# Two attention and state-space layer pairs on one core: one region of fixed order over the whole program, new order strings, six normalisations and some evictions on other engines

## The chip, the cores and the metric

The kernel runs on one core of a Trainium2 chip. The metric is device time in microseconds: 395.22 is the median of three runs of the kernel before (394.33 to 395.49). The core's engines are named as in the profile: PE (TensorE, matmuls; PEld are its weight loads), DVE (VectorE), ACT (ScalarE), POOL (GpSimd) and SP (SyncE, which here issues nearly all DMAs). Each engine works through a queue of its own, in order, and waits on semaphores for the others.

## What is computed

The input `x` is 1 x 2048 x 512. Four residual layers follow each other, attention A and convolution B by turns:

```python
x = x + A(layernorm(x))      # then  x + B(layernorm(x)), and both once more
# A: 32 heads of 16, every position attends to 8 positions, 2 apart, behind it
qkv = x @ wqkv
logits = einsum("bhsd,bhswd->bhsw", q, kg) * scale     # masked, softmax over w
o = einsum("bhsw,bhswd->bhsd", attn, vg) @ wo
# B: a state-space layer as a long convolution
P = exp(dt * A * l);  K = einsum("dn,dnl,dn->dl", C, P, dt * B).real
y = irfft(rfft(u, 2L) * rfft(K, 2L))[:L] + u * Dskip
```

Both A layers share their weights, and both B layers their kernel `K` and so its spectrum.

## The kernel before

The program has these stages, one after the other; the times in brackets are where DVE works on them in the profiled execution.

- **Generator**, `k_gen` (0.9 to 101.3 us). It builds the tables from which `K` comes: a complex number per state is squared again and again (`square` on ACT, L1087; `double` and `differ` on DVE, L1091 and L1094; tile `sq_z`), the powers are copied out in bf16 (L1105, L1107, L1111), products of tables are made on DVE (L1119) and summed on PE (L1277). Between these stand table steps on ACT (L661, L684), the first layernorm of layer 0 (row statistics L145 and L1163, application `ln_apply` L195 on ACT or L197 on DVE and POOL), transposes, and the k and q projections (L1215, evicted at L1220). It ends with three multiplications of q by k for the first block of rows (L342, tile `A_pr`), their sums over the head's lanes on PE (`lsum`, L350), the store of `K` to `kd_dram`, and a copy into `kT_ext` (L295).
- **Core of layer 0**, `LayerA.core` (to 185.1). For each block of four row tiles: `mult` on DVE (L342, 128x4096, tile `prod`), `lsum` on PE, row maximum `mx` on DVE (L414), exponential and normalisation on ACT; for each of the 16 row tiles: `pv_mult` on DVE (L472, tile `pav`), `pv_sum` on PE, `out_proj` on PE (L508). `pv_sum` has two forms: whole, 32 matmuls of 128x128 (L487), and split, 64 matmuls on halves of the rows (L497). The v projection is L398, evicted into `v_ext` on ACT (L400). A second, shifted copy of `v_ext` is made by DMA in two parts of two DMAs each (L403, L404), the first behind the eight even row tiles of v, the second behind the odd ones. Between these, events load `K` back in two halves (`k_rl0`, `k_rl1`, 18 DMAs each, L1366 and L1382), permute it (`k_part`, L1459, tile `k_perm`) and build sine tables that are stored to `g_dram` (L744).
- **FFT of layer 0**, `FftB.run` (to 236.6). Three stages of matmuls with an eviction each: `f1` (L811, tile `a1s`) and `f2` (L818) forward, for the kernel (`K`, `k`) and the data (`U`, `u`, evicted into `ub` on ACT, L869); `u_mult` on DVE multiplies spectra (L857); `i1` (L883 whole, L887 in halves; tile `z`) and `i2` (L931 to L937, and L911 to L918) go back and add to `x_sb`. Spectra of the kernel go to `kf_dram`. The evictions of f1, kernel f2 and i1 share one line, L800, and go to ACT or DVE.
- **Front of layer 1** (to 262.0): statistics, layernorm (tile `xn`), transposes (L271, evicted at L273) and k projection (L282, evicted at L285), then the **core of layer 1** (to 348.6), which loads DFT weights `w_sb` again (L596, 32 DMAs) when the event `w` is reached.
- **FFT of layer 1** (to 376.3) and **tail**: the stored spectra come back tile by tile into a ring (`kf_ring`, L847 and L849, three DMAs each); `pump` loads up to ten ahead of the multiplication that runs. `g_sb` (1 MB, L770) brings the inverse tables. The output is stored per block (L1555).

The order of the work is written out by hand. Each stage has a string in which every letter or token issues one operation from a list, and so sets its place in all queues that it uses: ORDERK for the generator, CORE0 and CORE1 for the cores, ORDER0, ORDERF and ORDER1 for FFT 0, front and FFT 1. In FFT strings the last letter of a token is the engine of the eviction or normalisation (A is ACT, D is DVE, G is POOL with DVE). In the cores `m` is a product, `l` its sum, `v` and `q` projections, `P` a `pv_mult`, `S` and `V` a split and a whole `pv_sum`, `O` an `out_proj`, `a` and `f` a normalisation on DVE and ACT; digits and some capitals call events (in CORE0 `1` and `6` load `k_rl0` and `k_rl1`, `2` to `5` store sine tables, `A` to `H` are the `k_part`s). ENGK and KROWS hold the engines of the generator's and the `k_part`'s copies. A string holds inside a `manual_schedule` region, for the engines that the region names; there are five such regions (L1427, L1466, L1488, L1495, L1549). Outside of them, and across their seams, a scheduler of the language orders the instructions: for example the loads that `open_mid` issues before FFT 1, and the place of the sums L350 at the end of the generator beside the v projections at the start of the core.

Of the kernel before, what the change touches and what calls it, by code (L numbers as in the profile page):

```python
# [1403 lines left out]
):  # L1404
    nc = tc.nc
    cpool = ctx.enter_context(tc.tile_pool(name="consts", bufs=1))
    dram = ctx.enter_context(tc.tile_pool(name="dram", bufs=1, space=bass.MemoryType.DRAM))
# [87 lines left out]
    with tc.manual_schedule(engines=MAN):  # L1495
        la.front_open()
        la.front_zero()
        ln, agg, pts, whole = {}, {}, {}, set()

        def front_pools():  # L1500
            fb.swap_psum()
            la.front_psum()

        def whole_stats(b):
            whole.add(b)
            for a in range(4 * b, 4 * b + 4):
                nc.vector.bn_stats(lnst["bn"][:, a, 0, :], x_sb[:, a, :])

        def aggr(b):
            agg[b] = lnp.tile([P, 4, 2], F32, name="ln_ag")  # L1510
            for a in range(4):
                nc.vector.bn_aggr(agg[b][:, a, :], lnst["bn"][:, 4 * b + a, 0:1 if b in whole else 2, :])

        def power(b):
            ln[b] = rstd_act(nc, lnp, agg[b][:, :, 1]), agg[b][:, :, 0], -1.0

        def norm(b, eng):
            la.front_apply(b, x_sb[:, b * 4:(b + 1) * 4, :], ln_end(nc, lnp, ln[b]), dict(both=["act", "dve"], mixed=["pool", "dve"]).get(eng, [eng] * 2) * 2)

        def transposes(b):  # L1520
            pts[b] = la.front_t(b)

        def last(*ops):
            def f():
                for op, *ix in ops:
                    front[op](*ix)
            return f

        front = dict(S=front_pools, h=lambda g, t: half_stats(nc, lnst, x_sb, t, g), H=whole_stats, a=aggr, p=power, n=norm, T=transposes,
                     E=lambda b, d, eng: pts[b][d](eng), P=lambda b, ft: la.front_k(b, ["act"] * 4, (ft,)),  # L1530
                     Q=lambda q, ft: la.qproj1(q, ft, la.qT[q], la.ps_pj, la.pj_tag), x=lambda b: la.front_ext(b, "dve"),
                     e=lambda ft: la.front_ext(3, "dve", ft))
        fb.run(ORDERF, None, more=front)
        la.front_close()
        fb.c_ps.close()
        fb.c_grp.close()
        krctx.close()
        ev = {"w": lambda: la.load_w2(w2_dram),
              "0": last(("P", 3, 0), ("P", 3, 1), ("x", 0), ("x", 2), ("P", 3, 2), ("Q", 0, 1), ("e", 0), ("Q", 0, 2)),
              "1": last(("P", 3, 3), ("Q", 0, 3)), "2": last(("e", 1), ("e", 2)), "3": last(("e", 3))}  # L1540
        la.core(x_sb, u, lnp, CORE1, ev)
# [6 lines left out]
    fb.open_mid()  # L1548
    with tc.manual_schedule(engines=MAN):  # L1549
        out_v = out.rearrange("b (p a) d -> p (b a) d", p=P)  # L1550

        def store(g, t):
            gs = slice(g * 4 * DQG, (g + 1) * 4 * DQG)
            ts = slice(t * 4, t * 4 + 4)
            nc.sync.dma_start(out_v[:, ts, gs], x_sb[:, ts, gs])  # L1555

        fb.run(ORDER1, u, store)
# [34 lines left out]
```

## Time and profile before

| what | value |
|---|---|
| three runs | 394.33, 395.22, 395.49 us |
| profiled execution, span | 393.9 us, clock 0.999 of full speed |
| PE busy | 324.1 us (82%) |
| DVE busy | 372.8 us (95%) |
| ACT busy | 331.1 us (84%) |
| POOL busy | 65.5 us (17%) |
| moved by DMA | 54.18 MB, 138 GB/s over the span |

Every duration below is from one profiled execution, whose span goes from its first instruction to its last. The runs are timed around the whole execution; their median lies 1.3 us above that span, their lowest 0.4. In the lines of groups, `x30 | 67.6, 2287 | 0.3 <-DMA` reads: 30 instructions, 67.6 us busy in all, 2287 ns each, 0.3 us of idle time of the engine just before them, most of which a DMA ended. A timeline's line gives the start, the length and the engine, the line of code, the operation, its tiles, and in brackets the idle time before it with what ended it. Instructions of one engine overlap a little: a DVE instruction's duration is longer than the distance to the next start.

### The profile page before, as it was taken

To read this page: it belongs to the slowest core of one execution; us is meant where nothing else is said; L and a number is where in the kernel's file an instruction comes from. 1 tells how busy PE (TensorE), PEld (TensorE's weight loads), DVE (VectorE), ACT (ScalarE), POOL (GpSimd) and SP (SyncE) were. 2 spreads that over 40 slices of the span, in tenths; PEclk is the share of its full clock that TensorE was granted. 3 is DMA by queue.
4 is the path that set the end of the run, shared out by engine and by line. 5 is a ranking of instruction groups with operands and counts; after the bars stand their busy time and mean duration, and the time that the engine had idled before them with its cause. 6 is when DMAs were issued, how large, how long until landed. Compare 5 with 4: busy or idle time off the path is not lost.

```text
span 393.9 us, 14769 instructions
## 1 busy us (share of the span) xinstructions
PE 324.1 (82%) x6451; PEld 231.5 (59%) x6499; DVE 372.8 (95%) x449; ACT 331.1 (84%) x568; POOL 65.5 (17%) x97
## 2 busy tenths in 40 slices
PE   3000258999999999999998899999999999998894
PEld 2000116756734676766887888543456676677894
DVE  6999999999989999999999989979999999989984
ACT  7999999997558799899999998574666779889992
POOL 9402960000280000010731201100000020000000
PEclk9999999999999999999999999999999999999999
DMA  7953810414027556277678634820253057604525
GB/s 209 396 155 50 83 53 3 106 28 108 9 66 198 128 168 176 61 228 235 215 265 300 216 110 110 300 62 2 73 141 96 3 170 222 195 13 155 171 68 152
DMA packets 68303, 54.18 MB, mean 138 GB/s; under 512 B 33545, under 2 KB 58670, under 8 KB 67982
## 3 DMA queue, kind: packets, MB, share of 16 engines
q1 hardware_dynamic: 66566, 48.70, 42.7%
q0 software_dynamic: 1664, 4.52, 3.1%
q8 instruction: 51, 0.84, 0.9%
q14 instruction: 14, 0.11, 0.1%
q10 hardware_dynamic: 8, 0.00, 0.0%
HBM read 30.15 MB, written 13.24 MB: 110 GB/s over the span
## 4 chain that ended last, share of the span: by engine, by line
PE 49%; DVE 21%; ACT 19%; issue 5%; DMA 2%; SPq 2%; POOL 1%; DVEq 0%; ACTq 0%; POOLq 0%
PE pq L398 7%; PE po L497 5%; PE pq L508 4%; PE pq L223 4%; PE pk L1277 3%; DVE A_t L1119 3%; ACT ub L869 3%; DVE B_t L1119 3%; PE L L354 3%; PE pp L282 3%; ACT a1s L800 3%; PE pp L1215 2%; DVE t L857 2%; SPq L596 2%; PE L L350 2%
## 5 line engine op out<-in xcount | busy, mean ns | idle before, releaser
L472 DVE TENSOR_TENSOR pav<-attn,v_ext 128x4096 bf16<-128x4096 bf16 (+1 forms) x34 | 72.3, 2160 | 0.3 <-DMA v_ext<-v_ext 0.3
L342 DVE TENSOR_TENSOR prod<-qT,kT_ext 128x4096 bf16<-128x4096 bf16 x29 | 65.6, 2288 | 3.0 <-PE L L350 2.1
L1119 DVE TENSOR_TENSOR A_t<-A_t,pow_t 128x1024 bf16<-128x1024 bf16 (+4 forms) x46 | 38.2, 873 | 0.2
L1205 PE MATMUL pt<-ident,x_blk 128*128 128x128 bf16 x64 | 6.0, 241 | 39.4 <-ACT x_blk L195 39.4
L508 PE MATMUL pq<-wop,oT 128*128 128x512 bf16 x121 | 31.5, 379 | 2.4 <-issue 1.9
L497 PEld LDWEIGHTS <-pav 64*128 64x128 bf16 x1728 | 26.9, 95 | 9.9 <-DVE pav L472 3.3
L869 ACT CAST ub<-pb 128x1024 bf16<-128x1024 f32 x32 | 32.6, 1110 | 0.0
L1215 PE MATMUL pp<-xnT,kT_ext 128*128 128x512 bf16 x88 | 25.5, 413 | 7.3 <-ACT xnT L1208 4.3
L818 PE MATMUL pb<-a1s,w_sb 128*128 128x64 bf16 x768 | 27.4, 193 | 3.8 <-ACT ub L869 1.4
L398 PE MATMUL pq<-wv,xnT 128*128 128x512 bf16 x123 | 30.0, 379 | 0.5 <-ACT kgs L1285 0.3
L497 PE MATMUL po<-ident,pav 64*128 64x64 bf16 x1728 | 29.9, 190 | 0.6 <-ACT oT L499 0.2
L400 ACT CAST v_ext<-pq 128x512 bf16<-128x512 f32 x32 | 18.7, 586 | 13.5 <-PE pq L398 11.1
L800 ACT CAST a1s<-pb 128x1024 bf16<-128x1024 f32 x29 | 28.5, 1063 | 1.2 <-PE pb L811 1.2
L1205 PEld LDWEIGHTS <-x_blk 128*128 128x128 bf16 x64 | 4.6, 107 | 41.3 <-ACT x_blk L195 40.2
L818 PEld LDWEIGHTS <-w_sb 128*128 128x128 bf16 x768 | 25.1, 98 | 6.0 <-issue 4.0
L178 POOL TENSOR_TENSOR ln_rstd<-ln_rstd,ln_mh 128x4 f32<-128x4 f32 x2 | 4.0, 1995 | 120.1 <-DVE ln_rstd L177 66.9
L1277 PEld LDWEIGHTS <-A_t 128*64 128x64 bf16 (+1 forms) x512 | 21.7, 103 | 3.8 <-DVE A_t L1119 0.2
L800 DVE CAST a1s<-pb 128x1024 bf16<-128x1024 f32 x19 | 22.5, 1220 | 1.4 <-PE pb L811 1.0
L1277 PE MATMUL pk<-B_t,A_t 128*64 128x84 bf16 (+1 forms) x512 | 23.5, 201 | 0.2
L223 PE MATMUL pq<-xnT,kT_ext 128*128 128x512 bf16 x85 | 22.6, 379 | 0.9 <-issue 0.5
L225 ACT CAST qT<-pq 128x512 bf16<-128x512 f32 x24 | 14.0, 585 | 9.8 <-PE pq L223 9.5
L398 PEld LDWEIGHTS <-xnT 128*128 128x128 bf16 x128 | 11.9, 97 | 15.3 <-issue 2.4
(264 smaller groups left out, 919.9 us busy)
## 6 DMA issues: line engine op xcount, KB each, us to landing
w_sb<-w_dram SPq DMA_DIRECT2D x64, 128.0 KB, 3.0
w_dram<-xnT SPq DMA_DIRECT2D x1, 4096.0 KB
kf_ring<-kf_dram SPq DMA_DIRECT2D x13, 256.0 KB, 3.8
kf_ring<-kf_dram SPq DMA_DIRECT2D x26, 128.0 KB, 3.6
v_ext<-v_ext SPq DMA_DIRECT2D x4, 784.0 KB, 6.1
x_blk<-in_A_x_dram SPq DMA_DIRECT2D x4, 512.0 KB, 4.7
kT_ext<-in_A_wqkv_dram SPq DMA_DIRECT2D x4, 512.0 KB, 9.2
x_sb<-in_A_x_dram SPq DMA_DIRECT2D x4, 512.0 KB, 6.3
```

The costliest lines, as they stand in the source:

```text
L223: nc.tensor.matmul(pq[:], lhsT=self.wqk[:, dt, ft * P:(ft + 1) * P], rhs=self.xnT[:, dt, q * 512:(q + 1) * 512], start=(dt == 0), stop=(dt ...
L342: nc.vector.tensor_tensor(pr, self.qT[q][:, ft].unsqueeze(1).to_broadcast([P, W, 4, P]), kap, ALU.mult)
L398: nc.tensor.matmul(pp[:], lhsT=xnT[:, dt, a * P:(a + 1) * P], rhs=wv[:, dt, :], start=(dt == 0), stop=(dt == NDT - 1))
L472: nc.vector.tensor_tensor(pv[:, i], attn[:, n % 4].unsqueeze(2).to_broadcast([P, W, DH // parts, H]), vap, ALU.mult)
L497: nc.tensor.matmul(po[:, h, 0, i * nt + ft, :], lhsT=pvf[rows, i, w, ft * P:(ft + 1) * P], rhs=ident[rows, rows], start=(w == 0 and ft + i ...
L508: nc.tensor.matmul(pw[:], lhsT=oT[:, ftp, :], rhs=self.wo[:, ftp, :], start=False, stop=(ftp == NDT - 1))
L800: (self.nc.scalar.copy if eng == "act" else self.nc.vector.tensor_copy)(dst, src)
L818: nc.tensor.matmul(p2[:, j, :], lhsT=self.w2[:, ec * EC + j, :], rhs=a1s[:, ec * EC + j, :], start=True, stop=True)
L869: nc.scalar.copy(ub[:], p2)
L1119: return lambda: nc.vector.tensor_tensor(*args)
L1215: nc.tensor.matmul(pps[kind, b, ft][:], lhsT=la.wqk[:, dt, c:c + P], rhs=la.xnT[:, dt, b * 512:(b + 1) * 512], start=(dt == 0), stop=(dt = ...
L1277: nc.tensor.matmul(o, lhsT=lhs, rhs=Bt[:, ri, c * CH + ql].rearrange("p b g -> p (b g)"), start=(not half and j % 4 == 0 and ri == 0), sto ...
```

## The change

One region of fixed order for DVE, ACT, PE and SP is opened at the start of the program and closed at its end. The five inner regions go; `k_gen` keeps one that adds POOL. All six strings are written anew. The number of operations stays; their engines change in some places:

- six normalisations of 128x512 go from DVE to ACT: two in the generator (`x_blk`: one in ENGK's `y`, one in `z`), four in the cores (`a` to `f`, into `xnT`);
- one transposed eviction (L273) goes from DVE to ACT; of the f1 evictions one `a1s` more is on ACT, and of the i1 evictions one into `xnT` goes to ACT and two into `z` to DVE; one `kf_sb` eviction goes to DVE;
- one power copy of the generator (ENGK's `b`, L1107) and one `k_part` (KROWS) go from ACT to DVE;
- five whole `pv_sum`s (`V`) become split ones (`S`), so that no whole one is left;
- in the order of SP: `k_rl0` stands before the second part of the `v_ext` copy and before three of the four `x_sb` loads; the stores to `g_dram` stand after `k_rl1`; in layer 1 `g_sb` and all of the `kf_ring` loads stand after the `v_ext` copies and the `w_sb` loads.

Both kernels issue 281 DMAs. Line numbers of the changed kernel are lower by two from the helpers on. The core of the diff (the rest is indentation):

```diff
-MAN_ALL = MAN | {ET.Pool}
...
 DQT = 8
 NQT = DQG // DQT
 ORDERK = """
-sbiCCiCisCGiCbiMsaibsCbMiibMcMsTibMGicGMMbasMGiGibTMTMbsGGTabbiTTiaTsicGTbbacTiTibcGsTMTGiaGaMlM
-TbasMlWaiaMlyMMwyyiMiayMsttbeMkTaaaMadeMaiMkkaMKMTalMbMkMlWMMqMKqlqMqMMMyyQMHQyqqUQkkpyakKaUkKqt
-pUtUxUexqpQUaekdkUqUUaxaqUKUpUUk3axHUl3EkplTKpTWQ3Tl3xlTxTyppWyqyqkHxTlytkTTQqUzzeKqUTteQUkTkTKE
-kUTzkzUkTxkTKttkKkUkUkpKekekxKUUpkkKqxpKUqUUxUkUoEUUkpQkUKkpxUUoxpUXpxXKopxxZXZZ
+sbiGCCiGCsGbGaiiMsMiGbiCiasCMbiCbsbMiMTibaMisbibMcciTbsMTcbiTcsbMbiGGTTiTMcTGaGTabaGaiGaaTMMTlsM
+MilaMwWlTMbMyyaMiyTMaMsyattieTaMeMaqMbkMdkMlsaiMKqMlMaiMaQkMaMMaaWqqMlkbQMMMKqaTyHqkQyyapkypkktx
+UaKpUUeUUUtKxUqeUlUqlUWUpUlQqqqyxqUQQHUTkdkKkkyTxp3yTpx3TxpT3Tp3yEHTlkTWUkUKtxTkUKkTtUeleUzKTkkK
+UTkqzzUqkUzKtkQtkTekkUTUKekxkppEKkUkxpUUKoxUKEqUUqUxopkUxkUQppXUKoxXpkkxKpxXZZZx
 """
 ORDER0 = """
-KD KA KA KA KA KD KD KA KA KD kA KD KA KD KA kA kD UA KD UA UD UA UA UD UA UD
-kA KD kA kD u kD u m u kA kD UA UA m u kD UA kD m UA UA u m kD UA m
-u u UD UA m u kA u m m kA kD kA m yD u m u YA m u YA yD u u m
-m YA u m u m w000A m YA yA YD YA yA yD yA w010D yA
+KA KA KA KD KA KD KA KD KA KA KD kA kD KA KD UA UA UD UA UD UA UD UA KD kA kA KD KA kD u kD u kA kD
+UA m UA kD m UA UA kD u UA u m kD UA u u m kD UA m u m u UD kA m kA u kA m kD m u m u yA YA YD m u u
+m yA u m u u w000A m YA YA m m yD YA YD yA yD yA w010D yA
 """
 LATE0 = "a s t g r b m"
 ORDERF = """
-yD h00 h01 yA YA v101A v100A v110A v111A h10 z12A a0 p0 v113A h11 a1 p1 z02A S z03A n0D T0 n1G E00D
-v103D E01A P03 H2 a2 T1 P01 E10D p2 E11D Q00 n2G H3 P00 a3 P02 P11 P12 p3 T2 E21D E20D P10 P13
-P22 P20 n3D T3 E31A P23 P21 E30D x1
+yD yA h00 YA v101A h01 v100A v110A h10 v111A a0 h11 z03A a1 p0 v113A z02A S n0D p1 z12A n1G T0 E01A
+E00D H2 v103D P01 Q00 T1 a2 E10A p2 E11D n2G P03 P13 P12 H3 P10 T2 a3 p3 P11 E20D E21A P00 n3D P02
+T3 P20 P23 E30D E31D P21 P22 x1
 """
 ORDER1 = """
-UD UA UA UD UA UD UA UD UA UD UA u UD m u m u u m UA u UA m u UD m
-UA m u m u u m u m u u m YA YD u YA m m yA YD m u u YA u YA
-YA m m m w001A w000D yA yA w011D YA w010D yA yD yA yD yA v102D v101A v112D v111A v113D v103D v100A v110D
+UA UD UA UD UA UA UD UA UD UA UD u UD UA m u UD m UA u u m u u m UA m u m u m u u m m u u m YD YA m
+YA u yD u YA m m YA m u u m YA m YA w001A w000D yD yA w011D YA w010D yA yD yA yD yA v102D v100A
+v112D v110D v113D v103D v101A v111A
 """
 
 CORE0 = """
-vmvvvvqlvmxvlmemvvrclvnlmqTlqmxmvvelvvvvcmlqcPlSPrqOmncml1VTxPPqeSmr2lqP4OlSOSm5PqOP3S7lmOSnlPOx
-VPeOPSPrOSnPO6SObbP9SwOP8SPdBHOVaOPfSEdObatSaCaAfataGDFO
+vvvmlvmvvmvlxlcmvqev1lcmrqlnmxmvqTvPevPvclvqcvvmlqmrlq6nlSqTmx8mPeSPOOSr34PqlSmO5PlSOl2m7PSlOnSx
+ePOSPbrPOSnPOdSfOPS9POSfOSbOPSPfBdfOPSDObaSaCAGHFttOaEwa
 """
 CORE1 = """
-0m1l2ml3mqvvmvllqvmqvxqelmlvmmvvqrlnqlmTvmxPPvlvvqvvqvmlmvqlqelmSrqnxmPSPqTOSOSlePOlPmrSOSnmOOPl
-bSlPSPwOxdfPVaePOSraPOnVabPOSPdOSOPSbPOSfaOftSdafaaftO
+0mv12mllmqvvvq3lmmlvvvqqmllxvmqeqmlvrlnvvmTmvvvlqqxvvPlPqmelqmlSmxrqnOSmPqTSPOPelSmlrOSPnlPOmSOP
+SOPlSwOxbSeOPrPSdnbOPSfOSOPSfadOPSPfObSfOfPSdtatafaOfa
 """
 ROWS0 = (0, 2, 1, 3, 4, 5, 6, 7, 8, 9, 10, 11, 12, 13, 14, 15)
 ROWS1 = (0, 2, 1, 3, 4, 5, 6, 7, 8, 9, 10, 11, 12, 13, 14, 15)
 NCOL = (2, 2)
-ENGK = dict(b="AAAAAAAAAAAAAAAAA", y="AAAAAAAAAADA", z="DAAA", e="AAAAAAAA", K="AAAAAAAAAAAAAAAA", Q="AAAAAAAA", x="AAAAAAAAAAAAAAAA")
+ENGK = dict(b="ADAAAAAAAAAAAAAAA", y="AAAAAAAAAAAA", z="AAAA", e="AAAAAAAA", K="AAAAAAAAAAAAAAAA", Q="AAAAAAAA", x="AAAAAAAAAAAAAAAA")
 STATD = (3,)
-KROWS = "DADAADDD"
+KROWS = "DDAADDDD"
 VROWS = (*range(0, 16, 2), *range(1, 16, 2))
...
     nc = tc.nc
+    ctx.enter_context(tc.manual_schedule(engines=MAN))
...
-    with tc.manual_schedule(engines=MAN_ALL):
+    with tc.manual_schedule(engines={ET.Pool}):
         C = k_gen(tc, nc, lambda sp: build_a_consts(nc, cpool, sp, consts), ins, kd, la, x_v, lnst,
...
-    with tc.tile_pool(name="ctmp_g2", bufs=1) as g2tmp, tc.manual_schedule(engines=MAN):
+    with tc.tile_pool(name="ctmp_g2", bufs=1) as g2tmp:
...
-    with tc.manual_schedule(engines=MAN):
-        late["."] = lambda: None
-        fb.run(ORDER0, u, k=kp, late=[late[c] for c in LATE0.split()])
+    late["."] = lambda: None
+    fb.run(ORDER0, u, k=kp, late=[late[c] for c in LATE0.split()])
...
     la.front_w()
-    with tc.manual_schedule(engines=MAN):
-        la.front_open()
+    la.front_open()
...
     fb.open_mid()
-    with tc.manual_schedule(engines=MAN):
-        out_v = out.rearrange("b (p a) d -> p (b a) d", p=P)
+    out_v = out.rearrange("b (p a) d -> p (b a) d", p=P)
...
```

More of the change, by code (lines that the diff above doesn't have):

```diff
@@ L1494 @@
     la.front_w()
-    with tc.manual_schedule(engines=MAN):
-        la.front_open()
[L1497 to L1541, printed above, removed]
@@ new lines, with front_pools, whole_stats, aggr @@
+    la.front_open()
+    la.front_zero()
+    ln, agg, pts, whole = {}, {}, {}, set()
+    def front_pools():
+        fb.swap_psum()
+        la.front_psum()
+    def whole_stats(b):
+        whole.add(b)
+        for a in range(4 * b, 4 * b + 4):
+            nc.vector.bn_stats(lnst["bn"][:, a, 0, :], x_sb[:, a, :])
+    def aggr(b):
+        agg[b] = lnp.tile([P, 4, 2], F32, name="ln_ag")
+        for a in range(4):
+            nc.vector.bn_aggr(agg[b][:, a, :], lnst["bn"][:, 4 * b + a, 0:1 if b in whole else 2, :])
@@ new lines, in power, with norm, transposes, last @@
+    def power(b):
+        ln[b] = rstd_act(nc, lnp, agg[b][:, :, 1]), agg[b][:, :, 0], -1.0
+    def norm(b, eng):
+        la.front_apply(b, x_sb[:, b * 4:(b + 1) * 4, :], ln_end(nc, lnp, ln[b]), dict(both=["act", "dve"], mixed=["pool", "dve"]).get(eng, [eng] * 2) * 2)
+    def transposes(b):
+        pts[b] = la.front_t(b)
+    def last(*ops):
+        def f():
+            for op, *ix in ops:
+                front[op](*ix)
+        return f
+    front = dict(S=front_pools, h=lambda g, t: half_stats(nc, lnst, x_sb, t, g), H=whole_stats, a=aggr, p=power, n=norm, T=transposes,
+                 E=lambda b, d, eng: pts[b][d](eng), P=lambda b, ft: la.front_k(b, ["act"] * 4, (ft,)),
+                 Q=lambda q, ft: la.qproj1(q, ft, la.qT[q], la.ps_pj, la.pj_tag), x=lambda b: la.front_ext(b, "dve"),
+                 e=lambda ft: la.front_ext(3, "dve", ft))
@@ L1542 @@
+    fb.run(ORDERF, None, more=front)
+    la.front_close()
+    fb.c_ps.close()
+    fb.c_grp.close()
+    krctx.close()
+    ev = {"w": lambda: la.load_w2(w2_dram),
+          "0": last(("P", 3, 0), ("P", 3, 1), ("x", 0), ("x", 2), ("P", 3, 2), ("Q", 0, 1), ("e", 0), ("Q", 0, 2)),
+          "1": last(("P", 3, 3), ("Q", 0, 3)), "2": last(("e", 1), ("e", 2)), "3": last(("e", 3))}
+    la.core(x_sb, u, lnp, CORE1, ev)
     la.close_logits()
@@ L1548, with store @@
     fb.open_mid()
-    with tc.manual_schedule(engines=MAN):
-        out_v = out.rearrange("b (p a) d -> p (b a) d", p=P)
[L1552 to L1557, printed above, removed]
+    out_v = out.rearrange("b (p a) d -> p (b a) d", p=P)
+    def store(g, t):
+        gs = slice(g * 4 * DQG, (g + 1) * 4 * DQG)
+        ts = slice(t * 4, t * 4 + 4)
+        nc.sync.dma_start(out_v[:, ts, gs], x_sb[:, ts, gs])
+    fb.run(ORDER1, u, store)
     fb.c_mid.close()
```

## The prediction

> **What bounds the kernel now.** I read the page first: busy shares, the slices, the chain.
>
> ```profile
> PE 324.1 (82%) x6451; PEld 231.5 (59%) x6499; DVE 372.8 (95%) x449; ACT 331.1 (84%) x568; POOL 65.5 (17%) x97
> ...
> PE   3000258999999999999998899999999999998894
> ...
> DVE  6999999999989999999999989979999999989984
> ...
> PE 49%; DVE 21%; ACT 19%; issue 5%; DMA 2%; SPq 2%; POOL 1%; DVEq 0%; ACTq 0%; POOLq 0%
> ```
>
> DVE is busy 372.8 of 393.9 us, yet the chain that ended last runs half over PE: two queues take turns. DVE's idle 21.1 us is all that a better order can give without less DVE work. About 3.5 lie before the first loads land and 5.2 behind its last instruction, so some 12 us are in reach. I listed every DVE gap from its timeline; the ones that matter: 1.57 us at 109.8, 1.07 at 232.8, 1.05 and 1.16 at 258 and 260.8, 1.2 in three at 271 to 283, 0.82 at 348.6, 2.1 in four behind 377. Stage by stage (windows view) PE has as little room as DVE:
>
> ```profile
> 230.00:240.00 10.00, 9.61 (x301) 9.06 (x299) 8.53 (x15) 9.58 (x12) 0.00 (x0) 1.00 0.32 97
> ...
> 250.00:260.00 10.00, 9.95 (x71) 5.50 (x71) 8.27 (x22) 6.94 (x13) 1.82 (x2) 1.00 0.74 251
> 270.00:290.00 20.00, 19.84 (x166) 9.19 (x167) 18.83 (x10) 12.13 (x20) 0.00 (x0) 1.00 0.34 85
> ```
>
> (columns: length; busy and count for PE, weight loads, DVE, ACT, POOL; clock; DMA.) From 250 to 290 PE is full and DVE waits: there DVE work saved gives nothing.
>
> **The change by place.** All sums are against the profiled execution, 393.9 us of span; the three runs' median is 395.22, so I add 1.3.
>
> DVE's step is a row's duration less some 85 ns where the next instruction is independent (2.288 for L342, starts 2.20 apart). DVE loses six norms of 128x512 (four into `xnT` at 0.415, two of `x_blk` at 0.406: 6 x 0.33 = 2.0), one L273 copy (0.678), one `a1s` and one `xnT` eviction (1.22 each). It gains two `z` evictions, one `kf_sb` (1.22 each), one `k_perm` copy (0.42) and one power copy L1107, f32 to bf16, 1024 elements. DVE never did that copy: its floor is 0.43 (L1069, f32, 512 elements), its ceiling 1.22 (casts of 1024 from PSUM); I take 0.60, nearest to L1069 with its fixed part paid once. Sum on DVE about -0.5 to -0.7; ACT gets the mirror, six norms at 0.81, the copies at 1.0.
>
> PE: five whole `pv_sum`s (L487, 32 matmuls, 1.80 by the 32 steps) become split ones (L497, 64 matmuls, 1.04): -0.76 each, three in the first core (-2.3), two in the second (-1.5).
>
> *Generator* (0.9 to 101.3; DVE 97.1 busy, idle 3.3, of which 0.2 after the start): DVE work -0.73; dependent neighbours on DVE, which cost about 0.11 each, fall from 19 to 13: -0.6. Against it: the new string puts table steps and row statistics (0.62+0.19) ahead of the squares on ACT. Summing both queues in the new order, `square` (1.04) ends up to 1.5 us after DVE has finished the level before; by the old order at most 0.5. The stalls sum to 0.8 to 1.1. Net 0 (-1.0 to +1.5).
>
> *Seam of generator and first core.* The timelines of DVE and PE show the largest gap in the middle:
>
> ```profile
> 107.91 0.29 DVE L295 COPY kT_ext<-kT_ext 128x508 bf16<-128x508 bf16 x1
> 109.78 4.50 DVE L342 TENSOR_TENSOR prod<-qT,kT_ext 128x4096 bf16<-128x4096 bf16 x2 [1.57 <-PE L L350]
> ```
>
> ```profile
> 105.77 0.62 PE L350 MATMUL L<-A_pr,ind 128*32 128x512 bf16 x8
> 106.64 1.67 PE L398 MATMUL pq<-wv,xnT 128*128 128x512 bf16 x6 [0.26 <-ACT kgs L1285]
> 108.25 0.61 PE L350 MATMUL L<-A_pr,ind 128*32 128x512 bf16 x8
> 108.79 0.39 PE L398 MATMUL pq<-wv,xnT 128*128 128x512 bf16 x1
> 109.11 0.62 PE L350 MATMUL L<-A_pr,ind 128*32 128x512 bf16 x8
> ```
>
> DVE cannot write the next product before the third logit sum frees the pool. Outside the old regions the scheduler slipped seven v matmuls between the sums. In the one region the string ends on Z Z, so PE runs L350 back to back: the last needs the multiplication's end (108.0) plus 0.55 plus the 0.2 that a release takes: gap about 0.45. **-1.1** (-0.5 to -1.2); the postponed 2 us of PE are covered by the -2.3 of the split sums.
>
> *First core*: DVE work +0.3 (one `k_perm` copy more). On SP, layer 0's load `k_rl0` (18 DMAs) now stands before the second pair of v_ext copies:
>
> ```profile
> 119.18 0.95 SPq L404 DMA_DIRECT2D v_ext<-v_ext  x1
> ...
> 124.37 0.59 SPq L1464 DMA_DIRECT2D x_sb<-in_A_x_dram  x1
> 131.70 0.64 SPq L403 DMA_DIRECT2D v_ext<-v_ext  x1
> 132.38 0.90 SPq L404 DMA_DIRECT2D v_ext<-v_ext  x1
> 133.33 4.29 SPq L1464 DMA_DIRECT2D x_sb<-in_A_x_dram  x3
> 137.66 0.61 SPq L1366 DMA_DIRECT2D k_rl<-kd_dram  x1
> 138.31 12.07 SPq L1382 DMA_DIRECT2D k_rl<-kd_dram  x17
> ```
>
> SP issues in order. `x_sb` block 0 ends near 123.9 (1.1 earlier than before); `k_rl0` takes 10.4 to 12.7 (12.7 here, 2.3 of it a wait), so the pair starts at 134.3 to 136.6 and lands 6.7 later (131.70 to 138.44 here): 141.0 to 143.4. DVE reaches the first multiplication that needs it after 13 large steps, three `mx` and a little, 108.7 + 13 x 2.2 + 3 x 1.135 + 0.2 = 140.9. Stall 0 to 2.5; I take 0.6, the low end, because SP idles from 125 to 131.7 and the queue has only 2.3 of wait to lose. **+0.9**.
>
> *FFT of layer 0* to its last u_mult: two evictions off DVE, one on, **-1.1**; ACT's work there is even (`a1s` +1, `kf_sb` -1). *Front of layer 1*: PE does about 28.5 us in 30.3, DVE's saved 0.6 becomes idle time, **-0.3** (0 to -1.8). *Second core*: DVE -0.65 and the 0.26 wait on v_ext; the 271-to-283 gaps stay because PE is full there, **-0.7** (0 to -1.5).
>
> *FFT of layer 1*: the scheduler had issued `g_sb` and seven kf_ring tiles early, between the regions (245.8 to 256.3 and 283 to 289.8). Now they come behind both v_ext copies and the 32 `w_sb` loads. Let T be the end of product 29, which releases the `w_sb` loads (316.5 here). After T SP needs 18.4 (`w_sb`, 316.6 to 335.0 here), the 1 MB `g_sb`, and 2.0 per ring tile: ten tiles are out near T + 39.6 (before, the tenth slot came free at T + 40.5). By the rows in DVE's new order the first u_mult ends at T + 37.8, so SP starts the last six about 2 us late, of about 3 us of slack (the last landed at 373.36, last u_mult began 376.3). **+0.2** (0 to +2). *Tail*: one `z` eviction moves from ACT onto DVE's own waits on PE (0.81, 0.56, 0.42), **-0.6** (0 to -1.0).
>
> Sum: 0 - 1.1 + 0.9 - 1.1 - 0.3 - 0.7 + 0.2 - 0.6 = **-2.7**: 391.2 of span, 392.5 in the runs' terms.
>
> [...] The split sums use tiles of 64 rows. In the trace the 64 steps take 1.04, the 32 whole ones 1.80, and weight loads at L497 wait on issue 3.1 us in 8 cases, 0.4 at most. [...]
>
> **Rivals.** (1) *Slower: v_ext behind k_rl0.* If `k_rl0` meets a full queue as the later loads do (`k_rl1` 12.4, `w_sb` 17.8 for 32), and each small DMA waits for the one eight before it, the pair lands at 145 to 147 and DVE, with the PV products next in its fixed order, stands 4 to 6 us at 141. The gains elsewhere (-3.3 without that term) are gone at a landing of 144.2. Against: few other loads run then. Price: 393.9 - 3.3 + 5.0 + 1.3 = 396.9; with ring tiles late too, 398.5. (2) *Slower: ACT in the generator.* Its queue runs behind from 20 to 40 us; if the late squares shift all tables (+1.5) and `z` and norms on ACT delay the front (ACT 9.6 of 10 at 230 to 240), +3.5 on my sum: 396. (3) *No change:* gaps reappear as PE supply. PE is 97 to 99% busy from 250 to 340; if front, second core and FFTs give nothing, what is left is seam and v_ext: about -0.4, 394.8. (4) *More:* favourable ends in seam, front, core and tail: -6, 389.2.
>
> **How the numbers follow.** About 0.3% (1.2 us) is what a measurement of this kernel can tell from no change: 394.0 to 396.4 is "same". Forecast with (4): 0.56. (3), and half-cancelled mixtures: 0.18. (1): 0.13, (2): 0.08, ring or an unforeseen wait of the new order: 0.05; together slower 0.26. The range goes from 389.0, the favourable ends, to 398.0, which takes in (1) without the ring.
>
> **What would show it.** Right: no L398 between the three L350 groups before the first `prod`, the gap there under 0.6; none of the 160 wide matmuls at L487 left, 2048 at L497; DVE busy 372 or a little less; its first v_ext wait under 2.6; idle in the tail under 1.5. Wrong: a DVE wait on DMA v_ext near 140 above 4; DVE waiting on `ws` L1087 by over 1.5 in sum; PE idle above 1 us around 235 to 260; `t` L857 waiting on DMA kf_ring behind 365.

## The result and the profile after

The changed kernel takes 402.1 us (median of four runs, 401.04 to 403.29) against 395.34 for the kernel before beside it: 1.0169 times as long, 95% interval 1.0139 to 1.0199. The forecast was 392.5, its range ended at 398.0. The profiled execution has a span of 400.3 us, 6.4 above that of before, and a time of 402.07. Page of the changed kernel:

```profile
PE 326.6 (82%) x6659; PEld 228.9 (57%) x6659; DVE 371.8 (93%) x445; ACT 332.4 (83%) x572; POOL 67.1 (17%) x97
...
PE   3000358989999939999998899999999999887894
...
DVE  6999999999999948999999999968999999889994
...
PEclk9999989999999988999999999999999999999999
...
PE 34%; ACT 19%; DVE 18%; SPq 12%; DMA 9%; issue 6%; POOL 1%; DVEq 0%; ACTq 0%; POOLq 0%
```

DVE does 1.0 us less work, as forecast, and stands 7.4 us more. The hole is in the slices: PE 3 and DVE 4 in the fifteenth, 140 to 150 us. The chain, which before held 2% of SP's queue and 2% of DMA, now holds 12% and 9%: the order of the loads sets the end. PEclk, full all through before, has two dips.

By stages of DVE (from the start of the first instruction of each to that of the next; differences to before in us):

| stage | forecast | changed kernel | e5 | e14 |
|---|---|---|---|---|
| generator | 0 | -1.05 | -0.09 | -1.06 |
| seam | -1.1 | -0.46 | -0.42 | -0.46 |
| first core | +0.9 | **+7.83** | +2.48 | +1.53 |
| FFT 0 to the last u_mult | -1.1 | -1.72 | -1.53 | -0.96 |
| front | -0.3 | +0.43 | +0.78 | +0.81 |
| second core | -0.7 | **+1.80** | +0.66 | +0.26 |
| FFT 1 | +0.2 | -0.05 | -0.04 | -0.37 |
| tail to DVE's end | -0.6 | -0.73 | -0.93 | -0.93 |
| sum | -2.7 | +6.05 | +0.9 | -1.2 |

(e5 and e14 are experiments below: the changed kernel with SP's order changed in two and in four places.) Part of these differences is work that crossed a border. One `A_t` product (0.60) stands behind the first `A_pr` now and so counts for the seam, not for the generator. Row statistics of 0.68 that stood behind the first DVE eviction of FFT 0 now stand ahead of it, in the first core. Like for like the generator gains 0.45 and the seam 1.06, the first core loses 7.15 and FFT 0 gains 1.04. Two rows carry the loss. The seam did what the forecast said (timelines of DVE, then of PE, changed kernel):

```profile
107.46 0.28 DVE L293 COPY kT_ext<-kT_ext 128x508 bf16<-128x508 bf16 x1
108.26 4.49 DVE L340 TENSOR_TENSOR prod<-qT,kT_ext 128x4096 bf16<-128x4096 bf16 x2 [0.51 <-PE L L348]
```

```profile
106.69 1.52 PE L348 MATMUL L<-A_pr,ind 128*32 128x512 bf16 x24
108.15 1.25 PE L396 MATMUL pq<-wv,xnT 128*128 128x512 bf16 x5
```

The 24 matmuls of the three sums run in one piece, and the gap is 0.51 where 1.57 stood. The first core is another matter (SP's timeline of the kernel before, of the changed kernel, then DVE's of the changed kernel):

```profile
115.52 0.63 SPq L541 DMA_DIRECT2D v_ext<-rows  x1
117.16 0.23 SPq L1443 DMA_DIRECT2D dskip<-in_B_Dskip_dram  x1
118.45 0.69 SPq L403 DMA_DIRECT2D v_ext<-v_ext  x1
```

```profile
118.48 0.23 SPq L1442 DMA_DIRECT2D dskip<-in_B_Dskip_dram  x1
118.82 0.63 SPq L539 DMA_DIRECT2D v_ext<-rows  x1
119.51 0.70 SPq L401 DMA_DIRECT2D v_ext<-v_ext  x1
120.26 0.95 SPq L402 DMA_DIRECT2D v_ext<-v_ext  x1
...
125.43 0.59 SPq L1463 DMA_DIRECT2D x_sb<-in_A_x_dram  x1
126.07 0.56 SPq L1364 DMA_DIRECT2D k_rl<-kd_dram  x1
126.67 12.24 SPq L1380 DMA_DIRECT2D k_rl<-kd_dram  x17
139.03 0.64 SPq L401 DMA_DIRECT2D v_ext<-v_ext  x1
139.71 0.92 SPq L402 DMA_DIRECT2D v_ext<-v_ext  x1
```

```profile
126.70 4.49 DVE L470 TENSOR_TENSOR pav<-attn,v_ext 128x4096 bf16<-128x4096 bf16 x2 [0.68 <-DMA v_ext<-v_ext]
...
139.06 2.27 DVE L340 TENSOR_TENSOR prod<-qT,kT_ext 128x4096 bf16<-128x4096 bf16 x1
147.02 6.69 DVE L470 TENSOR_TENSOR pav<-attn,v_ext 128x4096 bf16<-128x4096 bf16 x3 [5.69 <-DMA v_ext<-v_ext]
154.76 2.29 DVE L340 TENSOR_TENSOR prod<-qT,kT_ext 128x4096 bf16<-128x4096 bf16 x1 [1.05 <-PE L L352]
```

`k_rl0` holds SP from 126.07 to 138.9; the second v_ext pair goes out at 139.03, where before it went at 131.70, and lands at 146.94. DVE is ready at 141.33 and waits 5.69 us. For the first pair, which went out 1.06 later than before, it had already waited 0.68. The third wait, 1.05 for PE, follows from the long one, as the windows of these microseconds show (columns as in the prediction):

```profile
142.00:144.00 2.00, 1.33 (x7) 0.39 (x4) 0.00 (x0) 1.77 (x6) 0.00 (x0) 1.00 1.16 263
144.00:146.00 2.00, 0.00 (x0) 0.00 (x0) 0.00 (x0) 1.03 (x4) 0.00 (x0) 1.00 1.09 205
146.00:148.00 2.00, 0.00 (x0) 0.00 (x0) 0.98 (x1) 0.00 (x0) 0.00 (x0) 0.79 1.01 389
148.00:150.00 2.00, 0.63 (x24) 0.64 (x26) 2.00 (x2) 0.00 (x0) 0.00 (x0) 0.50 1.01 322
150.00:152.00 2.00, 2.00 (x56) 1.91 (x51) 2.00 (x2) 0.59 (x1) 0.00 (x0) 0.50 0.44 53
152.00:154.00 2.00, 2.00 (x16) 0.90 (x14) 1.71 (x1) 1.71 (x3) 0.00 (x0) 0.50 0.07 16
154.00:156.00 2.00, 2.00 (x95) 1.81 (x93) 1.24 (x1) 2.00 (x3) 0.00 (x0) 1.00 0.30 86
```

PE has nothing to do for 6.03 us, until 149.37; its granted clock is half from 147.2 to 154.0, and the split sum that takes 1.11 at full clock (at 154.66) takes 1.89. In the second core PE stops in the middle of a split sum, with nothing that the trace names:

```profile
346.27 1.05 PE L495 MATMUL po<-ident,pav 64*128 64x64 bf16 x60
348.80 0.23 PE L495 MATMUL po<-ident,pav 64*128 64x64 bf16 x4 [1.48 <-issue]
```

DVE waits 1.52 us for the `out_proj` (L506) behind it:

```profile
350.26 0.70 DVE L136 BATCH_NORM_STATS2 ln_bn<-pq 128x6 f32<-128x512 f32 x1 [1.52 <-PE pq L506]
```

Of the windows that stood for a full PE, the front still is one, five microseconds later:

```profile
230.00:240.00 10.00, 9.71 (x311) 9.19 (x312) 9.54 (x9) 9.44 (x11) 0.35 (x1) 1.00 0.36 110
...
260.00:270.00 10.00, 10.00 (x60) 5.03 (x59) 6.86 (x12) 6.78 (x12) 0.00 (x0) 1.00 0.00 0
270.00:290.00 20.00, 20.00 (x146) 8.35 (x145) 18.21 (x10) 11.06 (x20) 0.00 (x0) 1.00 0.16 42
```

### The profile page after: what moved, and what is told of

Same layout as the page of the kernel before. It is cut to its first block, busy times and chain, and to the rows that moved or that the text cites. A ratio compares the mean times of both kernels' runs of the same rounds, so it can differ in the third digit from the quotient of the medians.

```text
span 400.3 us, 15136 instructions
## 1 busy us (share of the span) xinstructions
PE 326.6 (82%) x6659; PEld 228.9 (57%) x6659; DVE 371.8 (93%) x445; ACT 332.4 (83%) x572; POOL 67.1 (17%) x97
## 3 DMA queue, kind: packets, MB, share of 16 engines
q1 hardware_dynamic: 66566, 48.70, 42.3%
## 4 chain that ended last, share of the span: by engine, by line
PE 34%; ACT 19%; DVE 18%; SPq 12%; DMA 9%; issue 6%; POOL 1%; DVEq 0%; ACTq 0%; POOLq 0%
PE pq L396 5%; PE pk L1275 5%; SPq L594 4%; DMA kf_ring<-kf_dram 4%; PE pp L280 3%; PE pp L1213 3%; PE pq L221 3%; SPq L847 3%; DVE B_t L1117 3%; DVE A_t L1117 3%; DVE pav L470 2%; ACT a1s L798 2%; DMA v_ext<-v_ext 2%; DMA x_sb<-in_A_x_dram 2%; PE L L348 2%
## 5 line engine op out<-in xcount | busy, mean ns | idle before, releaser
L495 PEld LDWEIGHTS <-pav 64*128 64x128 bf16 x2048 | 32.8, 96 | 18.5 <-DVE pav L470 9.8
L495 PE MATMUL po<-ident,pav 64*128 64x64 bf16 x2048 | 36.4, 192 | 7.9 <-DVE pav L470 6.0
L506 PE MATMUL pq<-wop,oT 128*128 128x512 bf16 x128 | 32.8, 379 | 0.0
L1213 PE MATMUL pp<-xnT,kT_ext 128*128 128x512 bf16 x96 | 26.7, 412 | 6.0 <-ACT kT_ext L1218 2.5
L497 ACT CAST oT<-po 128x512 bf16<-128x512 f32 x32 | 18.4, 574 | 10.9 <-PE po L495 10.7
L176 POOL TENSOR_TENSOR ln_rstd<-ln_rstd,ln_mh 128x4 f32<-128x4 f32 x2 | 6.0, 2982 | 124.5 <-DVE ln_rstd L175 124.5
L221 PE MATMUL pq<-xnT,kT_ext 128*128 128x512 bf16 x96 | 25.0, 390 | 0.0
L798 DVE CAST a1s<-pb 128x1024 bf16<-128x1024 f32 x18 | 21.3, 1218 | 1.6 <-PE pb L809 1.4
L223 ACT CAST qT<-pq 128x512 bf16<-128x512 f32 x24 | 14.1, 586 | 10.3 <-PE pq L221 10.2
```

What stands on the lines that cost most here:

```text
L221: nc.tensor.matmul(pq[:], lhsT=self.wqk[:, dt, ft * P:(ft + 1) * P], rhs=self.xnT[:, dt, q * 512:(q + 1) * 512], start=(dt == 0), stop=(dt ...
L495: nc.tensor.matmul(po[:, h, 0, i * nt + ft, :], lhsT=pvf[rows, i, w, ft * P:(ft + 1) * P], rhs=ident[rows, rows], start=(w == 0 and ft + i ...
L506: nc.tensor.matmul(pw[:], lhsT=oT[:, ftp, :], rhs=self.wo[:, ftp, :], start=False, stop=(ftp == NDT - 1))
L798: (self.nc.scalar.copy if eng == "act" else self.nc.vector.tensor_copy)(dst, src)
L1213: nc.tensor.matmul(pps[kind, b, ft][:], lhsT=la.wqk[:, dt, c:c + P], rhs=la.xnT[:, dt, b * 512:(b + 1) * 512], start=(dt == 0), stop=(dt = ...
```

## The experiments

Theory 1: the v_ext pair behind `k_rl0` is most of the loss. Theory 2: the rest comes from layer 1's loads, which run late and close together, and stop PE in the second core. Rival to both: the new strings, or the region as such, are slower. Each kernel was timed in five rounds beside the kernel before, whose medians there were 395.43 to 395.49. Between kernels that differ in SP's order alone, the orders of the other engines are the same instruction by instruction; only `k_rl0`'s move in e1 takes one small addition on DVE (0.27 us) with it. Each kernel has one profiled execution, and its stops of PE and low clock need not be those of the median; where its time lies over 1 us from the median, it is given.

**e1: k_rl0 back behind the pair** (CORE0 of the changed kernel).

```diff
-vvvmlvmmvvmlxlcmvqev1lcmrqlnmxmvqTvPevPvclvqcvvmlqmrlq6nlSqTmx8mPeS...OPS9POS
+vvvmlvmmvvmlxlcmvqevlcmrqlnmxmvqTvPevPvclvqcvv1mlqmrlq6nlSqTmxmPeS...OPS89POS
```

> The changed kernel with one SP block moved back: the load k_rl0 (and the small fix that needs it) stands behind the second part of the v_ext copy again, as it did before; PE's order is untouched. Theory 1 (the late v_ext pair is most of the loss): the 5.7 us wait of DVE on v_ext at 141.3, PE's 6 us without work and the 6.8 us at half clock behind it go together; 402.1 falls by 6.5 to 7.8, to 394.3 to 395.6. Rival (the wait only moves, to k_rl0 or to the weights of FFT 0 that now load 3 us later): at most 3 us are gained, 399 or more.

Measured 398.83 (396.57 to 401.14), ratio to before 1.0084 (1.0053 to 1.0116): 3.3 less, half of what theory 1 expected, and next to the rival's 399, though DVE waits neither for `k_rl0` nor for the weights, as the rival had it. At the first pair DVE waits 1.00 us in this profile; the long wait, at the second, is gone (DVE's timeline):

```profile
140.19 2.28 DVE L340 TENSOR_TENSOR prod<-qT,kT_ext 128x4096 bf16<-128x4096 bf16 x1
142.39 4.49 DVE L470 TENSOR_TENSOR pav<-attn,v_ext 128x4096 bf16<-128x4096 bf16 x2
```

and the first core is 5.2 us shorter. What took some of it back: the stop of PE in the second core is longer, 2.52,

```profile
342.44 1.05 PE L495 MATMUL po<-ident,pav 64*128 64x64 bf16 x60
346.01 0.23 PE L495 MATMUL po<-ident,pav 64*128 64x64 bf16 x4 [2.52 <-issue]
```

at the same place as in the changed kernel, after 60 of 64 matmuls. And the generator ran with PE at half clock from 54.5 to 64.7 us, with a wait of 0.94 on DVE. None of the edits touches the generator, yet this low clock lasts 3.4 us in the profiles of the changed kernel, e6 and e14, and 10.2 in those of e1, e4, e5, e7 and e13, whose generators are 0.8 to 1.1 us longer; so that much of a difference between two of these profiles is no effect of an edit.

**e2: the mirror**, the kernel before with k_rl0 early (CORE0 of before).

```diff
-vmvvvvqlvmxvlmemvvrclvnl...qOmncml1VTxPPqeS
+vmvvvvqlvmxvlmemvv1rclvnl...qOmncmlVTxPPqeS
```

> The mirror: the kernel before with nothing but k_rl0's 18 loads put ahead of the second v_ext pair and of three x_sb loads. Theory 1: the pair is issued near 137.8 and lands at 144.5 to 146, DVE waits 4 to 6 us at 140 and PE falls to half clock for some 7 us: 399.5 to 402. Rival (in the kernel before the stall is taken up by slack behind it): under 1.5 us, 395 to 396.7.

Measured 402.14 (400.49 to 402.89), 1.0155 (1.0126 to 1.0183): +6.7, and at the place named:

```profile
145.77 4.49 DVE L472 TENSOR_TENSOR pav<-attn,v_ext 128x4096 bf16<-128x4096 bf16 x2 [5.64 <-DMA v_ext<-v_ext]
```

PE is at half clock from 144.4 for 6.8 us. One letter in the kernel before makes a slowdown as large as that of the whole change. Theory 1 holds there at full size. In the changed kernel, which has other delays too, the same move is worth 3.3 (e1).

**e3: the region alone**, with the strings and engines of before.

```diff
+    ctx.enter_context(tc.manual_schedule(engines=MAN))
...
-    with tc.manual_schedule(engines=MAN_ALL):
+    with tc.manual_schedule(engines={ET.Pool}):
...
-    with tc.manual_schedule(engines=MAN):
...
```

> The kernel before with the one region alone: the old strings and the old engines. PE loses the seven v matmuls between the first logit sums (gap of 1.57 us to about 0.45: -1.1); SP gets g_sb and the ring loads behind v_ext and w_sb. Theory 2a (ring loads that run late and close together cost time at the end of the second core or in FFT 1): -1.1 + 1 to 2.5, 395 to 396.8. Theory 2b (late loads are hidden): 394.2.

Measured 398.86 (396.91 to 402.28), 1.0095 (1.0057 to 1.0132): +3.4, more than either theory. In the profiled execution (402.28) PE stops 2.79 us in the second core, while the ring loads run behind `g_sb` (SP, then PE):

```profile
336.42 0.43 SPq L769 DMA_DIRECT2D g_sb<-g_dram  x1
```

```profile
341.33 0.61 PE L496 MATMUL po<-ident,pav 64*128 64x64 bf16 x30
344.73 0.71 PE L496 MATMUL po<-ident,pav 64*128 64x64 bf16 x34 [2.79 <-issue]
```

And the seam's gain is given back: the seven v matmuls that no longer stand between the first sums stand ahead of the next ones.

```profile
108.91 4.49 DVE L341 TENSOR_TENSOR prod<-qT,kT_ext 128x4096 bf16<-128x4096 bf16 x2 [0.51 <-PE L L349]
114.88 1.23 DVE L413 TENSOR_REDUCE mx<-L 128x128 bf16<-128x1024 f32 x1 [1.48 <-PE L L324]
```

With the old CORE0 the seam is worth -1.06 and +1.48; the changed CORE0 avoids that wait.

**e4: e1 with SP alone left to the scheduler ahead of FFT 1**, so that g_sb and ring loads go early, as before.

```diff
-    ctx.enter_context(tc.manual_schedule(engines=MAN))
+    ctx.enter_context(tc.manual_schedule(engines=MAN - {ET.SP}))
+    reg = ExitStack()
+    reg.enter_context(tc.manual_schedule(engines={ET.SP}))
+    ctx.enter_context(reg)
...
     fb.ahead = 10
+    reg.close()
     fb.open_mid()
+    reg.enter_context(tc.manual_schedule(engines={ET.SP}))
```

> The first kernel of this set, with SP alone left to the scheduler at the seam ahead of FFT 1: g_sb and nine ring tiles go out early again, as before; PE, DVE, ACT and POOL keep their orders. In the changed kernel PE stands 1.48 us within a split sum at 347.3, with nothing that the trace shows to wait for, while ring loads keep the DMA engines 88% busy, and the end of the second core is 2.3 us late by it. Theory 2a (instructions reach PE late because loads crowd the DMA engines): 1.5 to 2.5 us below the first kernel. Theory 2b (PE's longer code alone, or the order at the end of the core): within 0.5 of it.

Measured 397.11 (395.13 to 400.46), 1.0052 (1.0026 to 1.0079): 1.7 below e1 by the medians, but the two intervals overlap. The trace is clearer: the second core takes 86.67 us against 89.27, and PE does not stop in it, as theory 2a says. SP issues `g_sb` and seven ring tiles ahead of `w_sb`, as before. In this profile (399.13) PE stops 0.57 and 1.15 us in the first core instead, falls to half clock, and DVE loses 2.8 us.

**e5: e1 with g_sb alone early**, its tile allocated ahead of the second core and handed to FFT 1, which no longer loads it; the ring loads stay late.

```diff
-0mv12mllmqvvvq3lmm...
+g0mv12mllmqvvvq3lmm...
...
+    g2ctx = ExitStack()
+    g2 = g2ctx.enter_context(tc.tile_pool(name="b1_g2", bufs=1, reuse_waits="tile")).tile([P, 2, 16, P], BF16, name="g2_sb")
+    ev["g"] = lambda: nc.sync.dma_start(g2[:], g2_dram[:])
     la.core(x_sb, u, lnp, CORE1, ev)
```

> The e1 kernel with g_sb's 1 MB load alone put at the start of the second core (its tile allocated there); the ring loads stay late, and no other engine's order changes. In e1 PE stands 2.52 us at 343.5 within a split sum; its next block of 16 KB of instructions, which the trace shows on a queue of its own, comes 6.3 us after the one before, 1.4 us before PE goes on, and right behind g_sb's issue. Theory g (the 1 MB burst holds up the block): the stall at the end of the second core goes, 1.5 to 3 us below e1, about 396.3. Theory r (any dense loads do, the ring's too): a stall of over 1 us stays, within 1 us of e1.

Measured 396.14 (394.73 to 399.82), 1.0021 (0.9998 to 1.0045): 2.7 below e1, as theory g said, and clear of e1's interval. The load goes out at 241.70, and PE's stop at the same instruction is 0.48:

```profile
342.30 1.05 PE L495 MATMUL po<-ident,pav 64*128 64x64 bf16 x60
343.83 0.23 PE L495 MATMUL po<-ident,pav 64*128 64x64 bf16 x4 [0.48 <-issue]
```

**e6: e1 with five whole sums late in the second core** (CORE1).

```diff
-...nbOPSfOSOPSfadOPSPfObSfOfP...
+...nbOPVfOVOPVfadOPVPfObVfOfP...
```

> The e1 kernel with the last but one five pv_sums of the second core whole again (32 matmuls of 128 instead of 64: half of PE's instructions, 0.76 us more of PE each), loads as in e1. Theory c (PE eats 256 instructions in 2 us of split sums, faster than blocks arrive beside the loads): the stall at 343.5 goes or falls under 1 us although g_sb and ring loads come as late as in e1; 396 to 397.5. Rival (the loads stall PE whatever it runs, or a semaphore does it): a stall of 2 us or more stays and the whole sums cost more, 399 to 401.

Measured 398.32 (396.31 to 399.74), 1.0063 (1.0036 to 1.0090): between the two expectations. The stop in the second core is gone although g_sb is late, so theory c is right on that; but the stage is no shorter (89.47): DVE now waits 0.57 us for a whole sum and 1.31 for ACT's `x_sb` near its end, and PE stops 1.45 and 0.90 us in FFT 0 in this execution (399.51). Whether the longer sums cause the 1.31 isn't shown.

**e7: e4 with the first five sums of the first core whole** (CORE0).

```diff
-...q6nlSqTmxmPeSPOOSr34PqlSmO5PlSOl2m...
+...q6nlVqTmxmPeVPOOVr34PqlVmO5PlVOl2m...
```

> The e4 kernel with the first five pv_sums of the first core whole. In e4's trace PE stands 0.57 and 1.15 us without a releaser at 147 and 155, falls to half clock for 6.8 us, and DVE loses 2.8 us. Theory c: these stalls and the low clock go; 394 to 395.5, and with that no slower than the kernel before. Rival (first core does not depend on it): 396.5 to 397.5.

Measured 398.37 (397.68 to 400.05), 1.0075 (1.0045 to 1.0104). The expectation failed, and the time lies above the rival's too: in the profile (400.05) DVE waits 1.51 us for a whole sum at 146.2, and PE stops elsewhere (1.53 at 167.2).

**e8: the kernel before with all sums split** (the first of five places; the others alike).

```diff
-...qOmncml1VTxPPqeS...
+...qOmncml1STxPPqeS...
```

> The kernel before with all five whole pv_sums split, nothing else. As forecast in the terms of the sum, PE is 3.8 us less busy and DVE sets the pace: 0 to -1 us, 394.5 to 395.5. Theory c gives a cost of its own (faster use of instruction blocks beside the loads of the first core): +0.5 to +2, with stalls of PE in split sums that nothing releases.

Measured 396.45 (394.19 to 398.67), 1.0028 (1.0005 to 1.0052): a loss of 1.0 if any, no gain. The steps are as summed (1.04 for 1.80), but DVE sets the pace there. The profiled execution (395.06) had no stop of PE without a releaser, so what costs the 1.0 isn't shown.

**e9: e3 with g_sb early** (the edit of e5).

> e3 (the kernel before in one region) with g_sb's load alone put at the start of the second core. Theory g: e3's stall of PE at 341.9 (2.79 us, half clock behind it, +4.5 us at the end of the second core) goes; left are the seam's -1.1 and ring loads that are late but hidden: 394.3 to 395, 4 below e3. Theory r (dense ring loads are enough): 396.5 or more.

Measured 396.81 (395.33 to 399.98), 1.0042 (1.0020 to 1.0065): 2.05 below e3, not 4, which is the time that theory r gave; the intervals just overlap. The stop is gone though the ring loads stay dense, as theory g says, and the second core takes 86.54 us, as before; the 1.48 at the seam stays, which the expectation left out. In this profile (398.47) PE also stops 0.59 and 0.63 us near 178 and 195.

**e10: the changed kernel with g_sb early** (the edit of e5).

> The changed kernel with g_sb's load alone at the start of the second core; k_rl0 stays ahead of the v_ext pair. Theory: the two causes add up. The second core ends 1.5 to 2.5 us earlier, the wait on v_ext at 141 stays at 5 to 6 us: 399.6 to 400.6. Rival (a stall somewhere else takes the place, as in e6 and e7): 401 to 402.

Measured 401.74 (400.22 to 402.50), 1.0145 (1.0120 to 1.0170): 0.4 less, not 1.5 to 2.5, and inside the noise; it is the rival's time. The second core is 0.8 shorter, PE's stop 0.69 instead of 1.48; the wait on v_ext is 5.65, and the first core is 0.65 longer in this execution, with a wait of 1.10 for ACT at 126.3. In the changed kernel itself the second cause is the small one.

**e11 and e12: the three FFT strings of the changed kernel** (ORDER0, ORDERF and ORDER1 as in the diff of the change), in e9 and in the kernel before.

> e9 with the changed kernel's ORDER0, ORDERF and ORDER1 (and so its evictions there); generator and cores as before. By DVE's stages of the changed kernel against before: FFT 0 -1.5 to -1.7, front +0.4 to +0.8, FFT 1 and tail -1.0: 1.5 to 2 us below e9, 392.5 to 393.5, which would beat both kernels. Rival (what the stages gain is lost to stalls of PE elsewhere): as e9.

> The kernel before in its five regions, with the changed kernel's ORDER0, ORDERF and ORDER1 only. If the strings of the FFT stages are what is good in the change: 1.5 to 2 us below the kernel before, 393.4 to 394; against e11 the region's seam (1.1) is missing, and the loads of layer 1 go early by the scheduler. Rival: no difference, 395 to 395.8.

Measured 397.29 (396.18 to 399.04), 1.0041 (1.0021 to 1.0062), and 395.82 (394.91 to 397.22), 1.0004 (0.9986 to 1.0022). Against before, the FFT 0 stage is 1.7 shorter in both (0.7 of it moved into the first core's stage, as said) and the tail 0.9, but front and second core grow by 0.4 and by 0.4 to 0.8, and e12's profile (397.22) had a wait of 1.82 on an input load at 71.9. e11's (396.19) still has the seam's 1.48. No gain that can be measured: the rivals hold.

**e13 and e14: dskip out of the way**, in e5 and in e4. In the changed kernel SP stands at this small load ahead of the `rows` copy and the first v_ext pair; in the kernel before it stood between the two.

```diff
-    nc.sync.dma_start(dsk[:], ins["Dskip"].partition_broadcast(1))
...
     def k_half_load(h):
+        if h == 0:
+            nc.sync.dma_start(dsk[:], ins["Dskip"].partition_broadcast(1))
```

> e5 with the small dskip load taken from ahead of the first v_ext pair and put beside k_rl0. In e5 SP stands at dskip until 119.9 and issues the first v_ext pair at 120.9, 2.5 us later than before; DVE waits 1.51 us for it at 127.0. Theory d (the rest of the first core's loss is this third place in SP's order): the wait falls to under 0.5, 395.0 to 395.4, about 1 us below e5. Rival (the pair waits for ACT's eviction of v, not for SP): as e5, 396.1.

> The same in e4, where the ring loads go early too. Theory d: about 1 us below e4's 397.1; if stalls of PE without a releaser in the first core set e4's time (e4's profile had 2.8 us of them), it stays at 396.5 to 397.5.

Measured 395.52 (394.36 to 396.89), 1.0003 (0.9984 to 1.0021), and 395.46 (392.86 to 397.39), 0.9998 (0.9973 to 1.0024). In e13 the pair goes out at 118.57 and DVE doesn't wait for it (SP, then DVE):

```profile
117.39 0.63 SPq L539 DMA_DIRECT2D v_ext<-rows  x1
118.57 0.69 SPq L401 DMA_DIRECT2D v_ext<-v_ext  x1
```

```profile
124.57 2.29 DVE L340 TENSOR_TENSOR prod<-qT,kT_ext 128x4096 bf16<-128x4096 bf16 x1
126.77 4.49 DVE L470 TENSOR_TENSOR pav<-attn,v_ext 128x4096 bf16<-128x4096 bf16 x2
```

The wait is gone as theory d said; e13 gains 0.6, which is within the noise, and e14 1.7, just clear of it, for the expected 1. SP now waits for ACT's eviction of v ahead of the pair (0.5 us), as it did before the change (1.0). With PE, ACT and POOL in the orders of the changed kernel, DVE's too but for the one addition, and SP's order changed in three places (e13: `k_rl0`, `g_sb`, `dskip`) or four (e14: the ring too), the time is that of before. None of the 14 beats the kernel before.

## Why the prediction was wrong

**The failed step** is the first core's "Stall 0 to 2.5; I take 0.6, the low end, because SP idles from 125 to 131.7". DVE's wait for the second pair was 5.69 us, with 1.05 more at half clock behind it and 0.68 for the first pair; the stage cost +7.8. `k_rl0` took 12.8 us (forecast 10.4 to 12.7, so just above the upper end). It began at 126.07, not 123.9, because the first pair went out 1.06 later than before, and not 1.1 earlier: SP stood until 118.48 at `dskip`, which waited 1.2 us for stores of `kd_dram` and now stands ahead of `rows` and the pair. In the kernel before it stood behind `rows`, and SP then waited for ACT. The change's part on SP doesn't list this move. The pair took 7.9 to land, not 6.7. So it landed at 146.94 and not at 141.0 to 143.4; DVE's arrival, 140.9 forecast, was 141.33. All three errors went the same way, and the low end was taken. SP's idle time was no cover: SP issued in its string's order, its slack went to `k_rl0`, which stood first, and the pair went out at 139.03, 0.12 behind the last of its loads. The forecast's own sign of being wrong, a DVE wait on v_ext near 140 above 4, is what came.

**The rival was named and underpriced.** "v_ext behind k_rl0" had the place, the landing (145 to 147; 146.94) and the wait (4 to 6; 5.69). It had a chance of 0.13, and its price stood on gains of 3.3 that were not there. It left out the half clock behind the wait, 1.05 us more, and the late first pair, 0.68.

**The second core**, -0.7 forecast, +1.8: the stop of PE in a split sum was in none of the lists. The forecast had asked only whether ring loads reach DVE in time, and they did: ten tiles were out at T + 42.3, not T + 39.6 (T is 323.9 here), but DVE waited only 0.23 us for the last one, and FFT 1 changed by -0.05 for +0.2. That PE could stop beside loads (2.52 us in e1, 0.48 in e5 with `g_sb` early) was not thought of.

**The gains that did come**: seam gap 0.51 for 0.45; FFT 0 -1.0 like for like, for -1.1; tail -0.7 for -0.6, with 1.6 less waiting and one `z` eviction more, as forecast; DVE's work -1.0 for -0.5 to -0.7. ACT's lateness in the generator cost DVE nothing (idle 3.32 for 3.34), so the stage gained 0.45 like for like, for 0. The front grew by 0.4 although DVE's idle time there fell by 0.2. The forecast had DVE's work 0.6 smaller there; it is 0.63 larger, mostly because one of the two added `z` evictions (1.22) stands in the front and only one L273 copy (0.68) left it. A reading was off too, without consequence: behind DVE's last instruction lie 4.8 us, not 5.2.

With SP's order changed in four places, these gains make -1.2 in e14's profile (394.55), and nothing in the median of its twelve runs (395.46; 0.9973 to 1.0024); so the forecast's -3.3 without the pair was also too large by at least 2.2. What makes e14's runs scatter over 4.5 us is open.

**The change from whole to half tiles** is not what makes split sums dear. At full clock they take 1.04 to 1.11 in every trace, and the step ahead of one is some 0.1 us longer: in the changed kernel four L506 matmuls step 0.96 ahead of a split sum (345.31 to 346.27) and 0.87 ahead of a matmul of the whole array (349.19 to 350.06). What the runs show against them is the stop of PE in the second core: 2.52 us within a split sum in e1, none in e6, where five sums are whole.

## What to carry to other kernels

Compare the queue that issues the loads as carefully as those that compute: list every load that is moved past, what it takes by the trace, and who waits for the one behind it; three moves on SP (`k_rl0`, `g_sb`, `dskip`: e13) took back 6.6 of the 6.7 us here. Where a sum has a bound from a queue's backlog, take the end at which all its parts are late together. And look at what a large load stands ahead of on PE: 1 MB issued just ahead of dense, finely cut matmuls cost 2.7 us in e1 and 2 in e3, where PE stopped for 2.52 and 2.79 (in the changed kernel 0.4, inside the noise). Compare stages only after asking which work crossed their borders.

## What the runs showed of the hardware

Stops of PE to which the trace gives no releaser go with the packets of one DMA queue. Queue q8, one of the two that the page of the profile calls instruction, carries 52 packets of 16,384 bytes in the changed kernel, one for about every 256 of PE's 13,318 matmuls and weight loads (51 in the kernel before, which has 320 fewer). For such stops after 100 us, PE's instructions up to the stop were counted, and the last such packet looked up:

```
kernel   goes on  idle   PE instructions so far (mod 256)   packet landed before PE goes on
changed  348.80   1.48   11186 (178)                        1.45 us
e1       142.88   1.33    2237 (189)                        1.50
e1       346.00   2.52   11186 (178)                        1.41
e5       343.82   0.47   11186 (178)                        1.26
e10      348.92   0.69   11186 (178)                        1.48
e4       156.21   1.15    3003 (187)                        1.72
e6       193.25   1.45    5051 (187)                        1.43
e7       239.93   1.08    7099 (187)                        1.43
e3       344.73   2.79   10669 (173)                        1.25
```

These are nine of 25 of 0.46 us or more in eleven kernels. All 25 have a remainder of 156 to 189 (why not one value is not shown), and all end 1.2 to 1.7 us after a packet lands. The author's estimate from these counts and times: a packet is a block of some 256 of PE's instructions (13,318 to 52 packets), and at these stops PE stands at the end of a block whose successor isn't there. The number of packets fits: if a block ends at each of these remainders, PE stands behind 44 blocks at the long stops of the changed kernel and e1, behind 12 at the 1.15 of e4 and 28 at the 1.08 of e7, and 43, 11 and 27 packets have landed by then. In e1 the packet starts at 343.6, 6.3 us after the one before and behind `g_sb`, issued at 337.3; with g_sb early (e5) at 341.4. PE had begun the block before (count 10,930) at 340.2 and 340.1, so the packet came 3.4 us behind that in e1 and 1.3 in e5; in e4, where the ring is early too, it came 0.8 behind it, and PE did not stop. The two longest stand in split sums, where 128 instructions run in 1.04 us, beside dense loads (DMA engines 99% busy from 342 to 344 in e1, 56% in e5). Which of the loads is ahead of a given block was tried for g_sb alone (e5, e9, e10); the stops in the first core move from run to run and were not traced to one load.

Half clock stood beside some of the stops. In the changed kernel it began 3.8 us into the 6.03 without work and lasted 6.8; behind e3's stop of 2.79 it lasted 3.4, behind e1's of 2.52 there was none, but behind a stop of only 1.15 in e4 (at 156.2) it lasted 6.8. So the length of a stop alone doesn't decide it; what does is open.
